# Loads in two gated bursts, w_tok's tail half first, and q of batch 1 permuted on GpSimd, in a sorted-attention and token-mixing kernel

## The chip, the cores and the metric

The kernel runs on one core of a Trainium2 chip. The metric is device microseconds of one execution. Before the change, 13 runs have a median of 261.09 us (260.26 to 266.6). The core's engines run side by side, each in its own program order, and wait for each other on semaphores: TensorE (PE) multiplies matrices into PSUM, VectorE (DVE) and ScalarE (ACT) work on SBUF and PSUM, GpSimd (POOL) works on SBUF and issues DMAs, SyncE (SP) issues DMAs.

## The reference, cut to what matters

There are 4 batches of 8 heads, 768 tokens and head dimension 64. Attention first mixes blocks of k and v with a matrix P, which five rounds of row and column normalisation of `exp(sort_net)` give, and then attends within each of 8 blocks of 96 tokens. Its output, 768 tokens by 512 channels, goes through a token-mixing step and a two-layer channel step.

```python
k_sorted = einsum('bhij,bhjcd->bhicd', P, k_b)        # and v likewise
attn = softmax(scale * q_b @ k_sb.T)                  # within a block
x = (attn @ v_sb)                                     # 768 x 512 per batch
tok = einsum('ts,bsd->btd', w_tok, alpha1 * x + beta1)
u = x + lam * tok
a2 = alpha2 * u + beta2
out = u + lam * (maximum(a2 @ w_ch1, 0) @ w_ch2)
```

## The kernel before, in words

Every engine's order of instructions is written out by hand (class `Engine`, line 56 on: what is issued through `pe`, `dve`, `act` and `pool` keeps its program order). Nearly all DMAs that load from HBM are issued by GpSimd[...]. They run as one stream, in the order in which GpSimd issues them. SP issues what is stored, the round trip of mixed v through a scratch in DRAM, and DMA transposes.

The opening works on batch 0. GpSimd issues q (two halves, `load_q0`), then k and v of the first four heads (`load_raw0`), k of the others, v of heads 4 and 5, half of w_tok (columns 0 to 383, `load_wtok(0)`), v of heads 6 and 7, the other half of w_tok, the three vectors lam, alpha1 and beta1 spread over all partitions, and then raw v of batch 1 (lines 171 to 190 and 812). Meanwhile VectorE and ScalarE make P (until 11.60 us), and TensorE turns q. Then four pairs of heads are mixed (`mix_k0`, `mix_v0`), scored (`sc0`) and applied to v (`pv0`), woven by hand.

w_tok has to be transposed. `sort_wtok(n, part)` (line 593) has GpSimd bring its columns into the order in which the blocks are cut, n being a pair of 128-wide groups: part 0 takes 96 columns of each group, from the columns 0 to 575, part 1 takes 32 of each, from the columns 576 to 767. `prep_wtok` (line 604) has TensorE turn a group, ScalarE and VectorE copying it out; `prep_rs` sums rows. Then `tok_part` multiplies the token products, six tiles of 128 tokens, `moe_scale` and `moe_rest` make u of it, `moe_turn` turns u, and `moe_h` makes the hidden layer, 16 tiles of 128 for each half of the tokens.

Batch 1 starts inside this: `mixes` mixes its v, `regroup_v` (line 378) sends it through DRAM into `Vs[1]` by two pairs of DMAs on SP, `mix_k(1)` mixes its k in three groups, and `turn_q(1, n)` (line 233) turns its q on TensorE, 12 transposes of 64 columns of weights for each pair of heads, with a copy on VectorE. These stand between tiles of `moe_h(0, 0)`. GpSimd then waits for `Vs[1]` by a small copy into the tile `gate` (line 902), and only then issues the loads of batch 2; the transposes of q of batch 2 follow on SP (`cross_q`, line 136). From there, `weave` fills the gaps between the steps of a batch's attention with channel products of the batch before (`moe_h`, `moe_ch`); `moe_a` does the next batch's token step, for which GpSimd makes u from x in `moe_rows` and `moe_start`. A tile u32 is one of 11 buffers, so a new one waits for the store of an old one.

Of the kernel before, what the change touches and what calls it, by code (L numbers as in the profile page):

```python
# [9 lines left out]
F16 = mybir.dt.float16  # L10
# [7 lines left out]
def kernel(  # L18
# [22 lines left out]
    B, H, S, D = q.shape  # L41
# [4 lines left out]
    NT = S // 128  # L46
    CT = C // 128
    HT = HID // 128
    BH = B * H
# [39 lines left out]
    def psb(shape, dtype, name):  # L89
        return psB.tile(shape, dtype, name=name, tag="psB")  # L90
# [11 lines left out]
    def load_raw(b, kv):  # L102
        src = (k, v)[kv]
        raw = att.tile([128, HB * D], F16, name=f"raw{kv}", tag=f"raw{kv}", bufs=2)
        for th in range(2):
            pool.dma_start(
                raw[th * 64:(th + 1) * 64, :],
                src[b].rearrange("h (j th t) d -> th (h j) (t d)", j=NB, th=2)[th],
            )
        raw_of[(b, kv)] = raw  # L110

    def load_raw0(kv, lo, hi):
        if lo == 0:
            raw_of[(0, kv)] = att.tile([128, H, 6, D], F16, name=f"raw{kv}", tag=f"raw{kv}", bufs=2)
        pool.dma_start(
            raw_of[(0, kv)][:, lo:hi, :, :], (k, v)[kv][0, lo:hi].rearrange("h (p x) d -> p h x d", x=6)
        )
# [25 lines left out]
    def prep_affine():  # L143
        pool.tensor_tensor(a1lB[:], a1lB[:], lamB[:], ALU.mult)
        pool.tensor_tensor(b1lB[:], b1lB[:], lamB[:], ALU.mult)
# [22 lines left out]
    def load_wtok(half):  # L168
        cols = slice(half * (S // 2), (half + 1) * (S // 2))
        pool.dma_start(wt16[:, :, cols], moe_w_tok[:, cols].rearrange("(tt p) s -> p tt s", p=128))  # L170

    load_raw0(0, 0, 4)
    load_raw0(1, 0, 4)
    load_raw0(0, 4, 8)
    load_raw0(1, 4, 6)
    load_wtok(0)
    load_raw0(1, 6, 8)
    load_wtok(1)
    ones16 = const([128, 1], F16, "ones16")
    pool.memset(ones16[:], 1.0)  # L180
    NV = 2
# [3 lines left out]
    b1lB = const([128, C], FT, "b1lB")  # L185
    lamB = const([128, C], FT, "lamB")
    gate = const([64, 2], F16, "gate")
    pool.dma_start(lamB[:], moe_lam.partition_broadcast(128))
    pool.dma_start(a1lB[:], moe_alpha1.partition_broadcast(128))
    pool.dma_start(b1lB[:], moe_beta1.partition_broadcast(128))  # L190
    W1p = const([128, CT, HID], BF, "W1p")
    W2p = const([128, HT, C], BF, "W2p")
    w1v = moe_w_ch1.rearrange("(ci p) n -> p ci n", p=128)
# [33 lines left out]
    def spin(n):  # L227
        src = ident16[:].unsqueeze(1).to_broadcast([128, 4, 128])
        for _ in range(n):
            pe.matmul(idle[:], ident16[:], src, start=True, stop=True)  # L230


    def turn_q(b, h4, copy):
        qps = psb([128, S], F16, "q_ps")
# [48 lines left out]
    def load_w1(gs):  # L283
        for g in gs:
            pool.dma_start(W1p[:, :, g * 512:(g + 1) * 512], w1v[:, :, g * 512:(g + 1) * 512])
# [302 lines left out]
    w_tokT = const([128, NT, S], F16, "w_tokT")  # L588
    rs = const([128, NT], FT, "rs")

    wtp = []

    def sort_wtok(n, part):

        if part == 0:
            wtp.append(moep.tile([128, NT, 2, 128], F16, name=f"wtp_{n}", tag="a2T", bufs=3))
        lo, hi, base = ((0, 96, 0), (96, 128, TAIL))[part]
        w = hi - lo
        pool.tensor_copy(
            wtp[n][:, :, :, lo:hi],  # L600
            wt16[:, :, base + 2 * n * w:base + (2 * n + 2) * w].rearrange("p t (k c) -> p t k c", c=w),
        )

    def prep_wtok(which):
        for ks in which:
            pst = psa([128, S], F16, "wtok_ps")
            for tt in range(NT):
                pe.transpose(pst[:, tt * 128:(tt + 1) * 128], wtp[ks // 2][:, tt, ks % 2, :], ident16[:])
            dst = w_tokT[:, ks, :].rearrange("p (kt x) -> p kt x", x=128)
            act.copy(dst[:, :, 0:96], pst[:, 0:TAIL].rearrange("p (kt x) -> p kt x", x=96))  # L610
            dve.tensor_copy(dst[:, :, 96:128], pst[:, TAIL:S].rearrange("p (kt x) -> p kt x", x=32))

    def prep_rs(rps, part):
        for ks in part:
            for kt in range(NT):
                pe.matmul(
                    rps[:, kt:kt + 1], w_tokT[:, ks, kt * 128:(kt + 1) * 128], ones16[:],
                    start=(ks + kt == 0), stop=(ks + kt == 2 * NT - 2),
                )
        if part[-1] == NT - 1:  # L620
            act.copy(rs[:], rps[:])

    u_of = {}
# [31 lines left out]
    def tok_part(b, kt):  # L655
        if b == 0 and kt == 4:
            pair = psa([128, 2, C], FT, "tok_ps")
            for n in range(2):
                tok_of[(b, kt + n)] = pair[:, n, :]
        elif (b, kt) not in tok_of:  # L660
            tok_of[(b, kt)] = psb([128, C], FT, "tok_ps")[:]
        for n, ks in enumerate((1, 4, 0, 3, 2, 5)):
            pe.matmul(
                tok_of[(b, kt)], w_tokT[:, ks, kt * 128:(kt + 1) * 128],
                x_of[b][:, ks, :], start=(n == 0), stop=(n == NT - 1),
            )
# [77 lines left out]
    def moe_h(b, hf, which=range(HT)):  # L744
        if (b, hf) not in hT_of:
            hT = moep.tile([128, HT, 384], BF, name="hT", tag=("big", "hT1")[hf], bufs=1)
            hT_of[(b, hf)] = [hT[:, m, :] for m in range(HT)]
        for m in which:
            hps = psb([128, 384], FT, "h_ps")
            for ci in range(CT):  # L750
                pe.matmul(
                    hps[:], W1p[:, ci, m * 128:(m + 1) * 128], a2T_of[b][hf][:, ci, :],
                    start=(ci == 0), stop=(ci == CT - 1),
                )
            act.activation(hT_of[(b, hf)][m], hps[:], AF.Relu)
            yield 0.65, None
# [27 lines left out]
    def run(units):  # L784
        for unit in units:
            advance(unit, 0.0)
        settle()
# [4 lines left out]
    def sc0(h4):  # L792
        pair = [psa([128, 2, 4, 128], FT, "sc_ps") for _ in range(2)]
        for g in range(2):
            score(0, h4, ((0, 1, 2, 6), (3, 4, 5, 7))[g], pair[g])
        for g in range(2):
            ets[(h4, g)] = emit_exp(pair[g])
# [11 lines left out]
    v_copy(0, dve.tensor_copy)  # L809
    v_copy(1, act.copy)  # L810
    next(big)
    load_raw(1, 1)
    sort_wtok(0, 0)
    sort_wtok(1, 0)
    load_w1((0,))
    for n, part in ((0, 1), (1, 1), (2, 0), (2, 1)):
        sort_wtok(n, part)
    load_w1((1,))
    prep_affine()
    load_w1(range(2, 4))  # L820
    load_raw(1, 0)
    sc0(0)
    for h4 in range(H4 - 1):
        turn_v0(h4, dve.tensor_copy)
        k_copy = mix_k0(h4 + 1)
        k_copy(0, act.copy)
        k_copy(1, dve.tensor_copy)
        if h4 > 0:
            pv0(h4 - 1, 0)()
        v_copy = mix_v0(h4 + 1)  # L830
        v_copy(0, dve.tensor_copy)
        v_copy(1, act.copy)
        if h4 == 0:
            next(big)
        sc0(h4 + 1)
        if h4 > 0:
            pv0(h4 - 1, 1)()
    turn_v0(3, dve.tensor_copy)
    pv0(2, 0)()
    prep_wtok(range(0, 1))  # L840
    pv0(2, 1)()
    prep_wtok(range(1, 2))
    pv0(3, 0)()
    prep_wtok(range(2, 4))
    pv0(3, 1)()
    prep_wtok(range(4, 6))
    mixing_matrices(1)
    rps = psb([128, NT], FT, "rs_ps")
    prep_rs(rps, range(4))
    moe_rows(0, (0, 1))  # L850
    moe_start(0, ())
    tok_part(0, 0)
    moe_scale(0, 0)
    prep_rs(rps, range(4, NT))
    mixes(1, 0)
    moe_rows(0, (2, 3))
    moe_start(0, range(4))
# [33 lines left out]
    mix_k(1, gs=(0,))  # L891
    run(moe_h(0, 0, range(9, 11)))
    mix_k(1, gs=(1,))
    run(moe_h(0, 0, range(11, 12)))
    turn_q(1, 0, dve.tensor_copy)
    run(moe_h(0, 0, range(12, 13)))
    mix_k(1, gs=(2,))
    for n in range(1, H4):
        run(moe_h(0, 0, range(12 + n, 13 + n)))
        turn_q(1, n, dve.tensor_copy)  # L900
    stack.close()
    pool.tensor_copy(gate[32:64, :], Vs[1][32:64, 0, 0:2])
    load_raw(2, 1)
# [10 lines left out]
    for b in range(1, B):  # L914
        if b == 1:
            fill = chain(moe_h(0, 1), moe_ch(0, 0), moe_ch(0, 1, (0,)))
            steps = [(0.2, lambda: mixing_matrices(2, psb)), (0.6, lambda: mixing_matrices(3, psb)), (0.6, lambda: None)]
            steps += attention_steps(1, 6.4, 0.3)
        else:
            fill = chain(moe_h(b - 1, 0), moe_ch(b - 1, 0), moe_h(b - 1, 1), moe_ch(b - 1, 1, (0,)))  # L920
            steps = [(g, lambda g=g, n=n: mix_k(b, gs=(n,))) for n, g in enumerate((0.6, 3.0, 3.0))]
            steps.append((3.8, lambda: None))
            steps += attention_steps(b, 5.3)
        weave(fill, steps)
        run(fill)
        moe_rows(b, range(5, NT))
        moe_a(b)
        run(moe_ch(b - 1, 1, (1, 2)))
        moe_affine(b, 1)
        if b < B - 1:  # L930
            moe_rows(b + 1, range(3))
        if b == 1:
            pool.tensor_copy(gate[32:64, :], Vs[0][32:64, 0, 0:2])
            load_raw(3, 1)
            load_raw(3, 0)
            load_q(3)
            cross_q(3, regroup[2])
        if b < B - 1:
            moe_rows(b + 1, range(3, 5))
# [33 lines left out]
```

## Time and profile before

The profiled execution took 262.57 us, of which the program's span is 260.8 us; the rest lies around it.

| engine | busy us | share of the span |
|---|---|---|
| TensorE matmul | 249.9 | 96% |
| TensorE weight load | 140.1 | 54% |
| VectorE | 147.3 | 56% |
| ScalarE | 131.6 | 50% |
| GpSimd | 94.2 | 36% |

The granted TensorE clock is 1.0 all through. The DMA moved 30.88 MB, at 118 GB/s on average over the span, and most of it in the first 66 us. Busy time of TensorE is pipelined: matmuls overlap a little, so 96% says that it seldom waits, not that it is at its peak. The chain of work that ended last gives TensorE 78% of the span, DMA 7%, VectorE 4%. In the time lines below, a DMA's row shows when it was issued and not when it landed.

### The profile page before, as it was taken

The numbers are of one execution on the slowest core, as the hardware profiler recorded it, in microseconds if no ns is written. First come the engines' busy times: TensorE is split into PE (matmuls) and PEld (weight loads), VectorE is DVE, ScalarE is ACT, GpSimd is POOL, SyncE is SP. The second block draws the span as 40 slices with busy tenths as digits, with TensorE's granted clock in tenths as the row PEclk, the third lists the DMA queues.
The fourth block names the chain that finished last, engine by engine and source line by source line (L and its number), as shares of the span: only waits on it lengthen the run. The fifth ranks groups of instructions, "written<-read, shape, count | busy, mean of one in ns | idle before, by whom it ended". The sixth has DMA issues, their size and how long they took to land.

```text
span 260.8 us, 5125 instructions
## 1 busy us (share of the span) xinstructions
PE 249.9 (96%) x2048; PEld 140.1 (54%) x2048; DVE 147.3 (56%) x324; ACT 131.6 (50%) x240; POOL 94.2 (36%) x103
## 2 busy tenths in 40 slices
PE   5988899999999989999999999999999999999993
PEld 2467745665545434654565445655665446545542
DVE  5868686592167969942626696734527963042033
ACT  3587588758623432673376542752573326505600
POOL 8525978000679098009530970222003700000000
PEclk9999999999999999999999999999999999999999
DMA  5999999999499734996995137951200341012012
GB/s 81 184 202 266 180 194 239 211 216 152 76 194 130 186 105 101 209 99 116 213 176 104 43 83 170 139 56 46 79 0 3 80 119 42 3 40 80 3 40 80
DMA packets 63127, 30.88 MB, mean 118 GB/s; under 512 B 48824, under 2 KB 58816, under 8 KB 63104
## 3 DMA queue, kind: packets, MB, share of 16 engines
q0 software_dynamic: 23712, 15.60, 41.3%
q1 hardware_dynamic: 39296, 14.90, 32.8%
q8 instruction: 16, 0.26, 0.4%
q10 hardware_dynamic: 96, 0.07, 0.1%
q14 instruction: 7, 0.06, 0.1%
HBM read 32.78 MB, written 8.65 MB: 159 GB/s over the span
## 4 chain that ended last, share of the span: by engine, by line
PE 78%; DMA 7%; DVE 4%; ACT 3%; POOL 3%; issue 2%; SPq 0%; POOLq 0%; DVEq 0%
PE h_ps L66 32%; PE ch_ps L66 30%; PE tok_ps L66 8%; DMA wt<-in_moe_w_tok_dram 7%; PE sc_ps L66 2%; PE x_ps L66 2%; DVE x L66 2%; ACT u L66 2%; PE k_ps L66 2%; POOL raw L66 1%; PE q_ps L66 1%; DMA out_dram<-u 1%; DVE u L66 1%; ACT vA L66 1%; PE v_ps L66 1%
## 5 line engine op out<-in xcount | busy, mean ns | idle before, releaser
L66 ACT ACTIVATE hT<-h_ps 128x384 bf16<-128x384 f32 x128 | 60.5, 491 | 59.5 <-PE h_ps L66 59.1
L66 PE MATMUL h_ps<-a2T,W1p 128*128 128x384 bf16 x512 | 88.9, 326 | 0.3 <-ACT a2T L66 0.2
L66 PE MATMUL ch_ps<-W2p,hT 128*128 128x512 bf16 (+2 forms) x400 | 86.9, 371 | 0.0
L66 PEld LDWEIGHTS <-W1p 128*128 128x128 bf16 x512 | 48.5, 98 | 31.9 <-issue 0.7
L66 PEld LDWEIGHTS <-hT 128*128 128x128 bf16 x400 | 37.6, 98 | 41.0
L66 DVE TENSOR_TENSOR ch_ps<-ch_ps,lamB 128x512 f32<-128x512 f32 (+2 forms) x25 | 16.9, 676 | 55.5 <-PE ch_ps L66 32.0
L66 POOL TENSOR_SCALAR u<-b1lB,rs 128x512 f32<-128x512 f32 x18 | 27.9, 1558 | 29.1 <-DMA out_dram<-u 28.9
L66 POOL TENSOR_TENSOR u<-x,u 128x512 f32<-128x512 f16 x22 | 24.9, 1162 | 31.1 <-DVE x L66 28.5
L66 PE MATMUL tok_ps<-x,w_tokT 128*128 128x512 f16 x144 | 33.2, 379 | 0.8 <-DVE u L66 0.8
L66 ACT ACTIVATE et<-sc_ps 96x768 f16<-96x768 f32 x32 | 24.0, 803 | 11.1 <-PE sc_ps L66 11.1
L66 PEld LDWEIGHTS <-w_tokT 128*128 128x128 f16 x180 | 15.0, 97 | 18.1 <-issue 1.5
L66 DVE CAST kT<-k_ps 64x512 f16<-64x512 f32 x30 | 20.6, 687 | 4.7 <-PE k_ps L66 4.3
L66 ACT CAST u<-u 128x512 f16<-128x512 f32 x24 | 14.6, 620 | 15.5 <-DVE u L66 15.5
L66 DVE RECIPROCAL recip<-x_ps 96x8 f32<-96x8 f32 (+1 forms) x32 | 6.3, 196 | 28.2 <-PE x_ps L66 28.1
L66 DVE TENSOR_TENSOR tok_ps<-tok_ps,a1lB 128x512 f32<-128x512 f32 x24 | 16.6, 696 | 4.2 <-PE tok_ps L66 4.1
L66 DVE TENSOR_TENSOR x<-x_ps,recip 96x512 f16<-96x512 f32 (+2 forms) x32 | 17.7, 555 | 1.1
L66 DVE TENSOR_TENSOR u<-tok_ps,u 128x512 f32<-128x512 f32 x24 | 15.8, 683 | 3.0 <-POOL u L66 2.7
L66 DVE TENSOR_TENSOR u<-ch_ps,u 128x512 f32<-128x512 f32 (+2 forms) x25 | 16.8, 670 | 0.9
L66 POOL DMA_DIRECT2D qn<-in_q_dram x16 | 14.0, 907 | 4.9 <-DMA raw<-in_v_dram 2.6
L66 PEld LDWEIGHTS <-et 96*128 96x128 f16 (+1 forms) x288 | 12.2, 105 | 2.7
L66 POOL COPY gate<-Vs 32x2 f16<-32x2 f16 x2 | 0.4, 176 | 35.7 <-DMA Vs<-vscr 35.7
L66 PE MATMUL x_ps<-Vs,et 96*128 96x65 f16 (+1 forms) x288 | 13.1, 197 | 0.0
(89 smaller groups left out, 183.4 us busy)
## 6 DMA issues: line engine op xcount, KB each, us to landing
out_dram<-u SPq DMA_DIRECT2D x23, 192.0 KB, 2.4
raw<-in_k_dram POOLq DMA_DIRECT2D x8, 384.0 KB, 10.9
raw<-in_v_dram POOLq DMA_DIRECT2D x7, 384.0 KB, 8.3
vscr<-vA SPq DMA_DIRECT2D x6, 384.0 KB, 5.2
Vs<-vscr SPq DMA_DIRECT2D x6, 384.0 KB, 8.4
W1p<-in_moe_w_ch_dram POOLq DMA_DIRECT2D x4, 512.0 KB, 10.5
W2p<-in_moe_w_ch_dram POOLq DMA_DIRECT2D x4, 512.0 KB, 16.0
qn<-in_q_dram POOLq DMA_DIRECT2D x4, 384.0 KB, 9.8
```

Source lines behind the costliest of these rows:

```text
L66: ins = getattr(self.eng, name)(*args, **kwargs)
```

## The change

On GpSimd's queue, only q and the first four heads of k and v are issued at once. A small copy that reads P (written by 11.60 us before) holds back the rest of k, two more heads of v, the second half of w_tok's columns and the last heads of v. A second one, which reads the exponentials of the second pair of heads, holds back the first half of w_tok's columns; the four sorts that need the second half alone come after its issue, then the three vectors, raw v of batch 1, the two other sorts, and W1. w_tok's groups are turned in the order 4, 5, 0, 1, 2, 3, and batch 0's token products and row sums follow this order. The mixing matrix of batch 1 is made in a PSUM bank of the other pool (`psb`).

q of batch 1, loaded as before, is copied by GpSimd into another order (`sort_q`, two copies, in a buffer under the tag of vA). `turn_qp` turns 128 columns of weights at a time, 6 transposes for each pair of heads. Two pairs are turned between tiles of `moe_h(0, 0)`, the two others in the first steps of the weave.

```diff
     load_raw0(0, 0, 4)
     load_raw0(1, 0, 4)
-    load_raw0(0, 4, 8)
-    load_raw0(1, 4, 6)
-    load_wtok(0)
-    load_raw0(1, 6, 8)
-    load_wtok(1)
...
-    pool.dma_start(lamB[:], moe_lam.partition_broadcast(128))
-    pool.dma_start(a1lB[:], moe_alpha1.partition_broadcast(128))
-    pool.dma_start(b1lB[:], moe_beta1.partition_broadcast(128))
+    def load_affine():
...

...
+    def sort_q(b):
+        qp_of[b] = att.tile([128, NT, H, D], F16, name="qp", tag="vA", bufs=1)
+        for hh in range(2):
+            hs = slice(4 * hh, 4 * hh + 4)
+            pool.tensor_copy(
+                qp_of[b][:, :, hs, :].rearrange("p kt h d -> p h kt d"), qn_of[b][:, hs, :, :]
+            )
+
+    def turn_qp(b, h4, copy):
+        qps = psb([128, S], F16, "q_ps")
+        for kt in range(NT):
+            pe.transpose(
+                qps[:, kt * 128:(kt + 1) * 128],
+                qp_of[b][:, kt, 2 * h4:2 * h4 + 2, :].rearrange("p h d -> p (h d)"), ident16[:],
+            )
+        copy(qT_of[b][:, h4, :, :].rearrange("p kt x -> p (kt x)"), qps[:])
...
-        for n, ks in enumerate((1, 4, 0, 3, 2, 5)):
+        for n, ks in enumerate((4, 5, 0, 1, 2, 3) if b == 0 else (1, 4, 0, 3, 2, 5)):
...
-    load_raw(1, 1)
-    sort_wtok(0, 0)
-    sort_wtok(1, 0)
-    load_w1((0,))
-    for n, part in ((0, 1), (1, 1), (2, 0), (2, 1)):
-        sort_wtok(n, part)
-    load_w1((1,))
-    prep_affine()
-    load_w1(range(2, 4))
-    load_raw(1, 0)
+    pool.tensor_copy(gate[0:BH, :], P16[:, 0, 0:2])
+    load_raw0(0, 4, 8)
+    load_raw0(1, 4, 6)
+    load_wtok(1)
+    load_raw0(1, 6, 8)
     sc0(0)
...
         sc0(h4 + 1)
+        if h4 == 0:
+            pool.tensor_copy(gate[0:64, :], ets[(1, 0)][0:64, 0, 0, 0:2])
+            load_wtok(0)
+            for n, part in ((2, 0), (2, 1), (0, 1), (1, 1)):
+                sort_wtok(n, part)
+            load_affine()
+            load_raw(1, 1)
+            sort_wtok(0, 0)
+            sort_wtok(1, 0)
+            load_w1(range(2))
+            prep_affine()
+            load_w1(range(2, 4))
+            load_raw(1, 0)
...
-    mixing_matrices(1)
+    mixing_matrices(1, psb)
...
-    run(moe_h(0, 0, range(11, 12)))
-    turn_q(1, 0, dve.tensor_copy)
-    run(moe_h(0, 0, range(12, 13)))
+    run(moe_h(0, 0, range(11, 13)))
     mix_k(1, gs=(2,))
-    for n in range(1, H4):
-        run(moe_h(0, 0, range(12 + n, 13 + n)))
-        turn_q(1, n, dve.tensor_copy)
+    sort_q(1)
+    run(moe_h(0, 0, range(13, 14)))
+    for n in range(2):
+        turn_qp(1, n, dve.tensor_copy)
+        run(moe_h(0, 0, range(14 + n, 15 + n)))
...
-            steps = [(0.2, lambda: mixing_matrices(2, psb)), (0.6, lambda: mixing_matrices(3, psb)), (0.6, lambda: None)]
+            steps = [(0.0, lambda: turn_qp(1, 2, dve.tensor_copy)), (0.6, lambda: mixing_matrices(2, psb))]
+            steps += [(0.6, lambda: turn_qp(1, 3, dve.tensor_copy)), (0.6, lambda: mixing_matrices(3, psb))]
             steps += attention_steps(1, 6.4, 0.3)
```

More of the change, by code (lines that the diff above doesn't have):

```diff
@@ L187 @@
     gate = const([64, 2], F16, "gate")
-    pool.dma_start(lamB[:], moe_lam.partition_broadcast(128))
-    pool.dma_start(a1lB[:], moe_alpha1.partition_broadcast(128))
-    pool.dma_start(b1lB[:], moe_beta1.partition_broadcast(128))
+    def load_affine():
+        pool.dma_start(lamB[:], moe_lam.partition_broadcast(128))
+        pool.dma_start(a1lB[:], moe_alpha1.partition_broadcast(128))
+        pool.dma_start(b1lB[:], moe_beta1.partition_broadcast(128))
     W1p = const([128, CT, HID], BF, "W1p")
@@ L230, in spin @@
             pe.matmul(idle[:], ident16[:], src, start=True, stop=True)
+    qp_of = {}
+    def sort_q(b):
[13 more added lines that the diff above has]
+        copy(qT_of[b][:, h4, :, :].rearrange("p kt x -> p (kt x)"), qps[:])
     def turn_q(b, h4, copy):
@@ L589 @@
     rs = const([128, NT], FT, "rs")
-    wtp = []
+    wtp = {}
     def sort_wtok(n, part):
-        if part == 0:
-            wtp.append(moep.tile([128, NT, 2, 128], F16, name=f"wtp_{n}", tag="a2T", bufs=3))
+        if n not in wtp:
+            wtp[n] = moep.tile([128, NT, 2, 128], F16, name=f"wtp_{n}", tag="a2T", bufs=3)
         lo, hi, base = ((0, 96, 0), (96, 128, TAIL))[part]
@@ L611, in prep_wtok, with prep_rs @@
             dve.tensor_copy(dst[:, :, 96:128], pst[:, TAIL:S].rearrange("p (kt x) -> p kt x", x=32))
-    def prep_rs(rps, part):
-        for ks in part:
+    def prep_rs(rps, part, first=False, last=False):
+        for n, ks in enumerate(part):
             for kt in range(NT):
@@ L617, in prep_rs @@
                     rps[:, kt:kt + 1], w_tokT[:, ks, kt * 128:(kt + 1) * 128], ones16[:],
-                    start=(ks + kt == 0), stop=(ks + kt == 2 * NT - 2),
+                    start=(first and n + kt == 0), stop=(last and n == len(part) - 1 and kt == NT - 1),
                 )
-        if part[-1] == NT - 1:
+        if last:
             act.copy(rs[:], rps[:])
@@ L839 @@
     pv0(2, 0)()
-    prep_wtok(range(0, 1))
+    prep_wtok((4,))
     pv0(2, 1)()
-    prep_wtok(range(1, 2))
+    prep_wtok((5,))
     pv0(3, 0)()
-    prep_wtok(range(2, 4))
+    prep_wtok((0, 1))
     pv0(3, 1)()
-    prep_wtok(range(4, 6))
-    mixing_matrices(1)
+    prep_wtok((2, 3))
+    mixing_matrices(1, psb)
     rps = psb([128, NT], FT, "rs_ps")
-    prep_rs(rps, range(4))
+    prep_rs(rps, (4, 5, 0, 1), first=True)
     moe_rows(0, (0, 1))
@@ L853 @@
     moe_scale(0, 0)
-    prep_rs(rps, range(4, NT))
+    prep_rs(rps, (2, 3), last=True)
     mixes(1, 0)
```

## The prediction

> **What bounds the kernel now.** I read the page's busy shares first, then the waits of TensorE after the opening, then the timeline around the one that matters, then the DMA by stretches. TensorE is busy for 96% of the span, and after 31 us it hardly waits. The list of waits (who, for whom: total us, times, longest us), TensorE only, from 30 us to the end, has four entries:
>
> ```profile
> PE tok_ps L66 <- DVE u L66: 0.8, 1, 0.8
> PE rep_ps L66 <- DVE w_tokT L66: 0.4, 1, 0.4
> PE h_ps L66 <- ACT a2T L66: 0.2, 1, 0.2
> PE wtok_ps L66 <- DVE w_tokT L66: 0.2, 1, 0.2
> ```
>
> So there are two regions: an opening of 31 us that waits for loads (the chain that ended last gives 17.54 us to the transfer of w_tok, up to 25.45), and a dense remainder with one hole of 0.77 us at 94.19. Whether a gain before 94 survives depends on that hole. The timeline (start, duration, engine, line, operation, tiles, [idle before <- releaser]) shows what ends it:
>
> ```profile
> 25.51 2.49 POOL L66 COPY wtp<-wt 128x384 f16<-128x384 f16 x4 [2.53 <-DMA wt<-in_moe_w_tok_dram]
> ...
> 48.87 0.61 PE L66 MATMUL k_ps<-bigP,raw 128*128 128x128 f16 x8
> ...
> 66.96 0.18 POOL L66 COPY gate<-Vs 32x2 f16<-32x2 f16 x1 [21.63 <-DMA Vs<-vscr]
> 67.49 1.08 POOL L66 DMA_DIRECT2D raw<-in_v_dram x2 [0.35 <-PE h_ps L66]
> ...
> 79.24 8.64 SPq L139 DMA_TRANSPOSE qT<-qn x6
> 87.98 0.52 SPq L763 DMA_DIRECT2D out_dram<-u x1
> ...
> 90.72 1.56 POOL L66 TENSOR_SCALAR u<-b1lB,rs 128x512 f32<-128x512 f32 x1 [6.45 <-DMA out_dram<-u]
> 92.25 6.78 POOL L66 TENSOR_TENSOR u<-x,u 128x512 f32<-128x512 f16 x6
> ...
> 94.19 2.75 PE L66 MATMUL tok_ps<-x,w_tokT 128*128 128x512 f16 x12 [0.77 <-DVE u L66]
> ```
>
> Read upwards. TensorE waits for VectorE's u, that for GpSimd's u at 92.25, which stands in program order behind the row at 90.72, which waits for a u buffer whose output is being stored. That store is issued at 87.98 only, because the six transposes of q of batch 2 stand before it on SP until 87.88. They began at 79.24, when that q landed, and its loads began at 67.49, after the gate on Vs of batch 1, landed at 66.82. From that landing to 94.19 it is 27.4 us of DMA, SP and GpSimd, none of which starts earlier when TensorE does. TensorE itself has 0.77 us to spare there.
>
> What sets 66.82? The DMA. By stretches (start:end, length, busy us of PE, PE's weight loads, DVE, ACT and POOL with their counts, clock, DMA share, GB/s written):
>
> ```profile
> 14.00:16.00 2.00, 1.63 (x38) 1.34 (x40) 0.85 (x3) 1.40 (x4) 0.54 (x1) 1.00 1.31 202
> 24.00:26.00 2.00, 1.23 (x28) 1.11 (x25) 1.59 (x6) 1.30 (x2) 0.49 (x2) 1.00 1.08 224
> 30.00:32.00 2.00, 1.64 (x34) 1.20 (x34) 1.50 (x7) 1.12 (x2) 2.00 (x3) 1.00 0.99 136
> 50.00:56.00 6.00, 6.00 (x72) 3.96 (x71) 5.86 (x10) 3.91 (x8) 0.00 (x0) 1.00 1.36 214
> ```
>
> The reader is to look at the last two columns: from 3 to 64 us the DMA has work without a break, and 202 GB/s, written as 16 bits from 32-bit sources, are some 404 GB/s read. The stream of loads is the second bound, running beside TensorE.
>
> **What the Trainium skill says.** *DMA: Bandwidth & Descriptors*, Specifications, puts the HBM limit of a core near 358 GB/s and the first byte of a GpSimd-issued transfer at about 1 us. The trace reads 404 GB/s, more than that; and from the issue at 67.49, with the DMA empty, its first packet starts at 68.73: 1.24 us. Its section Latency and other measured facts says that two of the sixteen DMA engines are usually slower. Agreed in kind: the trace's completion marks of v's first half come from thirteen engines at 12.1 to 12.7 and from three at 13.9 to 14.1. *GPSIMD Engine Reference*, 4.1, calls one-input operations roughly line rate; the sorts of w_tok agree (1.12 us for 1152 columns, 0.5 for 384). *TensorE: Matmul & The Clock Gate*, Part 4, gives some 275 ns for a transpose in context; here they stream at 0.67 us for 12 (uT_ps in the chain), 56 ns each, and the measurement decides.
>
> **The change part by part**, against the profiled execution (260.8 us of span, 262.57 us in all, so 1.8 us around it; the median of the runs is 261.09, 1.5 below this execution).
>
> *w_tok's order.* Now the first sort waits for w_tok's last half (25.45), and TensorE 0.84 us behind it. After, the tail half lands near 20 (its place in the stream: k's second half 1.95 us, v 0.97, w_tok 2.92, from 13.2). Sorts (2,0), (2,1), (0,1), (1,1): 1.12 + 3 x 0.5, done by 22.9. The sorts of the other half come after five DMA issues (3 x 0.55 + 2 x 0.53 = 2.7 us), 25.6 to 27.9, each before TensorE turns it, the turns taking 0.8 us apiece. So the first turn runs at 25.2 instead of 26.07: -0.87 us. ScalarE and VectorE, which copy each turn out (0.64 + 0.25), keep their pace. The bank of batch 1's mixing matrix moves from psA to psB, which ends the 0.36 us wait of rep_ps; the next token product waits for the last copy anyway: nothing.
>
> *q of batch 1.* 48 transposes of 49 ns (0.59 us for 12) become 24 of 56: 2.36 - 1.34 = -1.02 us on TensorE. VectorE's four copies stay (0.55 each), two of them moved into the weave. GpSimd gets two copies of 1536 columns, 1.4 us each by the sorts' slope, between q's landings (50.6, 52.6 now) and the first turn, about 4.8 us after the row at 48.87: 53.6. Cover is 1.6 us; without it, up to 1.4 us. They follow W2's issues and precede the gate on Vs, idle time (21.63 us) on GpSimd.
>
> So TensorE's own path gets 0.87 + 1.02 = 1.9 us shorter before 60 us, if no load is late. The product at 48.87 is the place to watch: its raw k landed at 48.73 (issued 33.21, longest landing 15.5). TensorE 0.87 earlier waits there for the same landing.
>
> *The two gates.* Each empties the stream. Gate 1 opens when P is done (11.60) and GpSimd has copied (0.2): issue at 11.9, first packet 1.24 later, 13.15. Thirteen engines ran dry near 12.0: 1.15 us x 13/16 = 0.93. Gate 2 (exp of head pair 1, about 18.5) lets the other half of w_tok out at 18.8, before the queue is empty: no gap. But behind it the affine vectors now stand after four sorts: issue 22.9, packet 24.1, while the stream ends near 22.9: 1.2 us on most engines, mean 1.0. Queued behind gate 2 on GpSimd are also raw v of batch 1, W1, the affine products and raw k. Raw v (landed 32.24, used 33.15, now wanted at 32.3) and the products (now 28.7 to 31.2, after some 29.7 to 32.2, wanted by VectorE at 32.2) just hold; W1 has 5 us in hand. k and v of gate 1's burst are wanted at 18.5 and later and land from 16. Sum +1.9 us of lost streaming. Unknown is what comes back, from 0 to all: the last engine ends Vs 1.1 us after the mean of the sixteen (65.73), and a pause lets laggards catch up, I take 0.6; the gather of Vs, issued up to 0.9 us earlier, has some 170 packets more beside W2 at 190 per us, of the 1000 per us it does alone: 0.2; the thin stretch 30 to 36 us (136 GB/s in the row above) may fill, 0 to 1.2: 0.2. I get 1.9 - 1.0 = +0.9, ends -0.7 and +1.9.
>
> *Sum.* Vs lands at 67.7, TensorE resumes near 95.1 instead of 94.19, and all after is dense: 260.8 + 0.9 = 261.7 of span, 263.5 for this execution, **262.0** on the median. The 1.9 us of TensorE become a longer wait there.
>
> **The rivals.**
> 1. *Stream on time*: laggards give everything back, Vs lands within 0.5 us of now. For: the engines that set each landing are the late ones, which the gaps don't stop. Against: 404 GB/s is a shared limit, so idle engines are lost bytes. TensorE's gain is absorbed at 94.19: 261.1.
> 2. *Faster*: evening out is worth more than the gaps cost. The mechanism is the same landing of Vs, and it decides from 66.0 down: each us earlier is a us of the end, until TensorE's own 0.77 + 1.9 is used up. For: w_tok's last engine came 1.5 us after the fifteenth (25.4, 23.9). With Vs at 65.4: 259.7.
> 3. *Slower by more*: raw k or q of batch 1 also land late (the permute then stands open, 1.4), and TensorE passes its slack: Vs +1.9 and 0.3 on top, 263.3.
> 4. *The gates do nothing*, queue never empty: as 1, for three engines it is so.
>
> **How the numbers follow.** Forecast 0.45, rival 3 0.10, rivals 1 and 4 0.25, rival 2 0.20. A difference under 0.3% (0.8 us) can't be told from none here: slower 0.55, same 0.25, faster 0.20. The forecast's own range is 261.9 to 262.9; with half of rival 2 and most of rival 3, 259.6 to 263.5.
>
> **What would show it.** Right: DMA share falling near 12 and 23 us; first wtok_ps near 25.2; q_ps of batch 1 x6; gate on Vs after 67.3; the wait of tok_ps near 95 grown to 2 us or more. Wrong: Vs by 66.0, or that wait gone; or a new TensorE wait on raw k, q or the affine vectors before 60 us that exceeds 2.7 us.

## The result and the profile after

The changed kernel takes 266.12 us (median of 11 executions, 264.63 to 267.58). Beside the kernel before, with a median of 261.81 in 48 executions, it is slower by 1.65%: ratio 1.0165, 95% interval 1.0138 to 1.0191. The prediction (262.0 us, 259.6 to 263.5) had the sign and the place of the loss, but forecast 0.9 us, where some 4.3 came. The profiled execution took 265.63 us with a span of 263.9, against 262.57 and 260.8: 3.1 us. The medians differ by more, because the profiled execution before took longer than the median of its kernel and the one after less. The two traces are therefore used for where the time goes, and the ratios for how much.

The four longest waits of TensorE from 30 us to the end (who, for whom: total us, times, longest us), changed kernel:

```profile
PE v_ps L66 <- DMA raw<-in_v_dram: 2.2, 1, 2.2
PE tok_ps L66 <- DVE u L66: 2.0, 1, 2.0
PE h_ps L66 <- DVE qT L66: 0.3, 1, 0.3
PE k_ps L66 <- DMA raw<-in_k_dram: 0.3, 1, 0.3
```

The hole before tok_ps, 0.8 before, has grown to 2.0. The prediction had named 2 us or more as a sign of being right, but by luck: it let the hole grow because TensorE comes early, and TensorE came late. Above the hole stands a wait for what the prediction said would "just hold": TensorE waits 2.2 us for raw v of batch 1. The timeline of the changed kernel (start, duration, engine, line, operation, tiles, [idle before <- releaser]), the rows that answer to those shown of before:

```profile
11.67 0.17 POOL L66 COPY gate<-P 32x2 f16<-32x2 f16 x1 [6.58 <-DVE P L66]
...
21.82 2.48 POOL L66 COPY wtp<-wt 128x1152 f16<-128x1152 f16 x4 [2.24 <-DMA wt<-in_moe_w_tok_dram]
24.25 0.57 POOL L66 DMA_DIRECT2D lamB<-in_moe_lam_dram  x1
...
70.10 0.18 POOL L66 COPY gate<-Vs 32x2 f16<-32x2 f16 x1 [13.31 <-DMA Vs<-vscr]
...
82.18 8.81 SPq L139 DMA_TRANSPOSE qT<-qn  x6
91.09 0.53 SPq L779 DMA_DIRECT2D out_dram<-u  x1
...
93.83 1.56 POOL L66 TENSOR_SCALAR u<-b1lB,rs 128x512 f32<-128x512 f32 x1 [6.66 <-DMA out_dram<-u]
```

```profile
35.49 0.59 PE L66 MATMUL v_ps<-raw,bigV 128*128 128x512 f16 x2 [2.23 <-DMA raw<-in_v_dram]
...
51.44 0.61 PE L66 MATMUL k_ps<-bigP,raw 128*128 128x128 f16 x8 [0.27 <-DMA raw<-in_k_dram]
...
97.29 2.75 PE L66 MATMUL tok_ps<-x,w_tokT 128*128 128x512 f16 x12 [1.96 <-DVE u L66]
```

The gate on Vs of batch 1 moved from 66.96 to 70.10, SP's transposes from 79.24 to 82.18, the store behind them from 87.98 to 91.09, GpSimd's sixth row from 90.72 to 93.83, and the token product behind the hole from 94.19 to 97.29: 2.9 to 3.1 us, and 3.1 is also the growth of the span. The chain that the prediction read from Vs to the hole kept its length and came 3.1 us later.

Where the loads lost it, by stretches (start:end, length, busy us of PE, PE's weight loads, DVE, ACT and POOL with counts, clock, DMA share, GB/s written). Of the kernel before, the stretch that the prediction did not show:

```profile
12.00:14.00 2.00, 1.56 (x17) 0.62 (x16) 0.97 (x3) 1.36 (x4) 0.54 (x1) 1.00 1.27 196
```

And of the changed kernel, to be set against that row and, for 14 to 16 and 24 to 26 us, against the 202 and 224 GB/s of the prediction's rows:

```profile
12.00:14.00 2.00, 1.93 (x36) 1.12 (x34) 0.74 (x3) 1.19 (x4) 2.00 (x3) 1.00 0.53 37
14.00:16.00 2.00, 1.73 (x47) 1.46 (x43) 1.34 (x4) 1.98 (x4) 0.79 (x2) 1.00 1.12 166
...
24.00:26.00 2.00, 2.00 (x54) 1.95 (x50) 1.65 (x5) 1.85 (x3) 2.00 (x5) 1.00 0.56 109
...
28.00:30.00 2.00, 1.48 (x28) 1.39 (x29) 1.18 (x4) 1.24 (x3) 2.00 (x3) 1.00 0.89 117
```

Both holes are there. Gate 1's costs (196 - 37) x 2 + (202 - 166) x 2 = 390 KB, 2.0 us at 195 GB/s; the second, before the vectors, leaves 109 of 224. A third thin stretch, 28 to 30 us, is the time in which the vectors land. The completion marks of the sixteen DMA engines give their mean: heads 6 and 7 of v at 21.6 instead of 19.7, the last half of w_tok 25.1 instead of 22.7, raw v of batch 1 34.4 instead of 28.8, Vs 69.3 instead of 65.7. For the last engine, which releases the waiting one, these are 22.8 (20.9), 27.0 (25.4), 35.4 (32.2) and 70.0 (66.8).

### The profile page after: what moved, and what is told of

The parts are those of the page before. It is cut to its first block, busy times and chain, and to the rows that moved or that the text cites. A ratio compares the mean times of both kernels' runs of the same rounds, so it can differ in the third digit from the quotient of the medians.

```text
span 263.9 us, 5084 instructions
## 1 busy us (share of the span) xinstructions
PE 249.4 (95%) x2024; PEld 140.1 (53%) x2024; DVE 147.4 (56%) x324; ACT 131.6 (50%) x240; POOL 97.6 (37%) x107
## 4 chain that ended last, share of the span: by engine, by line
PE 74%; DMA 10%; DVE 7%; POOL 4%; issue 2%; ACT 1%; POOLq 0%; SPq 0%; DVEq 0%
PE ch_ps L66 29%; PE h_ps L66 28%; PE tok_ps L66 7%; DMA raw<-in_k_dram 6%; DMA wt<-in_moe_w_tok_dram 3%; PE spin_ps L66 3%; DVE kT L66 3%; PE sc_ps L66 2%; PE x_ps L66 2%; DVE x L66 2%; PE k_ps L66 1%; POOL W1p L66 1%; ACT et L66 1%; PE q_ps L66 1%; DVE ch_ps L66 1%
## 5 line engine op out<-in xcount | busy, mean ns | idle before, releaser
L66 DVE TENSOR_TENSOR ch_ps<-ch_ps,lamB 128x512 f32<-128x512 f32 (+2 forms) x25 | 16.9, 676 | 53.9 <-PE ch_ps L66 30.4
L66 POOL TENSOR_TENSOR u<-x,u 128x512 f32<-128x512 f16 x22 | 24.9, 1162 | 31.5 <-DVE x L66 28.8
L66 PE MATMUL tok_ps<-x,w_tokT 128*128 128x512 f16 x144 | 33.2, 379 | 2.0 <-DVE u L66 2.0
L66 ACT CAST vA<-v_ps 128x1024 f16<-128x1024 f32 x9 | 9.1, 1011 | 7.3 <-PE v_ps L66 7.3
```

The lines of the kernel that those rows point to most:

```text
L66: ins = getattr(self.eng, name)(*args, **kwargs)
```

## The experiments

Two theories were to be told apart. A: holes in the stream of loads make Vs of batch 1 late, and the end follows it through stores and GpSimd's rows. B: TensorE's own waits before 62 us set the end. And within A, which of the parts makes the holes.

**Gates out, one at a time and both.**

```diff
-    pool.tensor_copy(gate[0:BH, :], P16[:, 0, 0:2])
...
-            pool.tensor_copy(gate[0:64, :], ets[(1, 0)][0:64, 0, 0, 0:2])
```

e1 leaves out the first of these lines, e2 the second, e3 both.

> The changed kernel without the copy that reads P: the second burst is issued at about 5 us, as before the change, w_tok's other half still waits for the exponentials. Theory A (the DMA stream loses what the gates and the jam of the three vectors cost, and the end follows the landing of Vs of batch 1 through the stores and GpSimd's rows): the empty stretch at 12 to 14.5 us cost 2 us of the sixteen engines' mean, so Vs lands 1.0 to 2.0 us earlier than 69.96 (68.0 to 69.0), and the ratio to the kernel before falls from 1.0165 to about 1.010. Theory B (gate 1 only evens the engines, the loss is all behind gate 2): Vs within 0.5 us of 69.96, ratio 1.015.

Measured: ratio 1.0111 (1.0052 to 1.0169). In its profile Vs landed at 69.54, only 0.4 us earlier, and TensorE waited 3.85 us for raw v of batch 1, with 0.71 left in the hole. The ratio is the one that A gave, but four executions leave an interval that overlaps the changed kernel's; that gate 1 counts is settled by e14 below. The landing forecast for Vs was missed. Of raw v the mean of the engines came 1.4 us earlier (32.97), and the last engine not (35.32 against 35.36). The profiled execution is the slowest of the four, so its waits overstate the loss.

> The changed kernel without the copy that reads the exponentials: w_tok's first half is issued behind gate 1's burst at about 15 us; the three vectors still stand behind four sorts. Theory A: the gate itself costs nothing, since the queue was not empty when it opened at 18.7; the hole at 24 to 25.5 us comes from the sorts ahead of the vectors and stays, so Vs within 0.5 us of 69.96, ratio 1.014 to 1.017. Theory B (the second gate is the loss): Vs at 68 or earlier, ratio 1.008 or less.

Measured: 1.0171 (1.0114 to 1.0227), Vs at 69.75, as A had it. Beside gate 1, gate 2 has no cost that four executions can show.

> The changed kernel without both gates, its order of loads, sorts, vectors and the permute of q kept. Theory A: without gate 1 w_tok is complete near 25, the vectors are issued after the sorts, near 24, and the hole before them shrinks; Vs at 67.5 to 68.5, ratio 1.006 to 1.010. Theory B (gates are the whole loss): Vs at 66.8 or earlier, ratio 1.000 or below, since TensorE's shorter q turns count.

Measured: 1.0102 (1.0071 to 1.0133), Vs at 68.53, the upper end of what A gave. With no gate at all a full per cent remains. The loss can't be the gates alone.

**The permute of q alone, on the kernel before.** Its edit is the permute's part of the change.

> The kernel before with the permute of q of batch 1 alone (two GpSimd copies, 24 transposes instead of 48, the new places of the turns). Theory A: TensorE gets 1.0 us shorter before 62 us, but the hole at 94 us takes it up, 0.77 growing to 1.5 to 1.8; the time stays, ratio 0.998 to 1.002. Rival (TensorE's own path sets the end): ratio 0.996, the hole unchanged. Rival (the permute is late and TensorE waits for it): a wait of q_ps on GpSimd's qp of over 0.5 us near 55.

Measured: 1.0013 (0.9985 to 1.0042): no change. In its profile, however, there is no hole at 94 at all, where one of 1.5 to 1.8 was expected; Vs landed at 65.64 there, and TensorE had lost 2.1 us between 21 and 28 us in two waits that no semaphore explains, beside 16 KB instruction fetches that began at 18.84 and 25.86. What these waits are is not shown. That the permute alone makes no difference is shown; that the hole absorbs the gain isn't shown by this trace.

**The end taken off the landing of Vs.**

```diff
     def moe_a(b):
...
-        moe_start(b)
+        if b == 1:
+            moe_start(b, range(5))
+            moe_rows(b, (5,))
+            moe_start(b, (5,))
+        else:
+            moe_start(b)
...
-        moe_rows(b, range(5, NT))
+        if b > 1:
+            moe_rows(b, range(5, NT))
         moe_a(b)
```

> The changed kernel with one edit far from the change: in batch 1's token step GpSimd adds x to five rows of u before it makes the sixth row, which waits for a store, so that the hole near 97 us no longer hangs on the landing of Vs. Theory A (the end follows Vs through stores and rows): the hole of 1.96 goes, and the end comes 1.5 to 2.0 us earlier, ratio about 1.009; what is left is TensorE's own lateness from raw v of batch 1. Rival (TensorE's own waits before 62 us set the end): no change, 1.0165, the hole only moves or stays.

Measured: 1.0092 (1.0067 to 1.0117), span 261.1. The waits of TensorE from 30 us on in this run are all but one small (the three longest):

```profile
PE v_ps L66 <- DMA raw<-in_v_dram: 1.6, 1, 1.6
PE h_ps L66 <- DVE qT L66: 0.3, 1, 0.3
PE h_ps L66 <- ACT hT L66: 0.2, 1, 0.2
```

The tok_ps row is gone, although Vs landed as late as before (69.67). So 0.7%, some 1.9 us, was what the chain from Vs cost beyond TensorE's own path, as A had it. The 0.9% that this edit doesn't touch agrees with lateness of TensorE's own: in this trace, the shortest of 20 executions, its first scores of batch 1 come at 61.42, 1.3 us later than before. A holds, and B stands right behind it; the prediction had B at nil.

> The kernel before with the one edit in batch 1's token step alone (five rows of u get x before the sixth row is made). If the hole at 94 us hangs on the landing of Vs through stores and rows, it goes and with it 0 to 0.8 us, according to how large it is in the run: ratio 0.997 to 1.000. If the hole has another cause it stays and the ratio is 1.000.

Measured: 1.0006 (0.9982 to 1.0030); no hole, with Vs at 65.16. On the kernel before the edit makes no difference that can be measured, so what e9 gained is not a gain of the edit by itself. That Vs is mostly early enough there for the hole to cost little would explain it; the other executions have no trace that shows it.

**The vectors and raw v of batch 1.** In e5 and e6 the vectors are issued right behind w_tok's first half; e6 leaves out both gates as well.

```diff
             load_wtok(0)
+            load_affine()
             for n, part in ((2, 0), (2, 1), (0, 1), (1, 1)):
                 sort_wtok(n, part)
-            load_affine()
```

> The changed kernel with the three vectors issued straight behind w_tok's first half, ahead of the four sorts (at 19.6 us instead of 24.25); raw v of batch 1 still behind the sorts. Theory A (hole and jam of the vectors behind the sorts are the larger part of the loss): no hole at 24 to 25.5, b1lB lands near 28.5 instead of 31.36, raw v of batch 1 near 33 instead of 35.36, TensorE's wait for it falls from 2.23 to under 0.7, Vs at 68 to 68.7, ratio 1.008 to 1.011. Rival (gate 1 is all that matters): raw v and Vs within 0.5 us of the changed kernel's, ratio 1.015 or more.

Measured: 1.0117 (1.0022 to 1.0212). The interval holds both answers, and the profiled execution (269.30 us) is the slowest of the four and is not read. Inconclusive by itself.

> The changed kernel with both gates out and the vectors ahead of the sorts: what is left of the change is the order of w_tok's halves, raw v of batch 1 behind four sorts, and the permute. Theory A: the stream has no hole any more, Vs at 66.8 to 67.5, TensorE waits for raw v under 0.5 us, ratio 1.000 to 1.004. Rival (the order of w_tok's halves or the permute costs something itself): ratio over 1.006.

Measured: 1.0000 (0.9970 to 1.0030), Vs at 66.12, even earlier than expected, no wait for raw v, which landed at 30.00. This is the decisive run: the order of w_tok's halves and the permute of q, which it keeps, together cost nothing, and the whole loss lies in when the loads are issued. Against e3 only the place of the vectors differs: without gates, vectors behind the sorts cost 1.0%. Its waits show what the prediction had expected of the changed kernel:

```profile
PE tok_ps L66 <- DVE u L66: 1.6, 1, 1.6
PE k_ps L66 <- DMA raw<-in_k_dram: 1.2, 1, 1.2
```

TensorE waits for raw k of batch 1 near 48, still comes to batch 1's first scores 1.3 us earlier than before (58.91), and the hole takes the gain.

> The changed kernel with the three vectors' tiles filled from 128 different rows of the second channel matrix each, instead of one row read 128 times: the same bytes, the same issues, another result (the affine part is left out and replaced by these numbers). If all engines reading one row at once is what makes the third vector take 2.5 us, it lands within 1.3 us of the second, raw v of batch 1 near 33.8, TensorE's wait for it under 1.0, ratio about 1.011. If it is the refilling of an empty queue, or anything else, the vectors land as before (27.8, 28.8, 31.4) and the ratio stays at 1.0165.

Measured: 1.0160 (1.0094 to 1.0226). The third vector landed 1.46 us after the second instead of 2.54, at 29.3 instead of 31.4: most of what the theory of one row had (under 1.3). But the last engine of raw v landed at 34.78, TensorE waited 1.88 us, and the time did not move by anything that four executions can show. So reading one row from everywhere does slow the third vector, and is not the main part of what makes raw v late.

> The changed kernel with raw v of batch 1 issued ahead of the three vectors, both still behind gate 2 and the four sorts. The theory that raw v, queued behind the vectors, makes TensorE's own lateness: raw v lands near 31.5 instead of 35.36, TensorE does not wait for it (under 0.4 instead of 2.23), mixed v is stored about 2 us earlier; but the vectors come 3 us later, near 33.5, their products on GpSimd near 36, and VectorE's first scaling of a token product waits for them, so that TensorE stands still for PSUM instead: ratio 1.014 to 1.020. Rival (raw v's place does not matter, only the bytes lost): Vs and the ratio unchanged within 0.2%, with no new wait.

Measured: 1.0188 (1.0135 to 1.0241). Raw v landed at 32.23 and TensorE didn't wait for it. The wait moved to VectorE, which stood still for the products of the vectors (timeline of this run, VectorE):

```profile
34.76 0.70 DVE L66 TENSOR_TENSOR tok_ps<-tok_ps,a1lB 128x512 f32<-128x512 f32 x1 [2.04 <-POOL a1lB L66]
36.38 1.42 DVE L66 SCALAR_TENSOR_TENSOR u<-b1lB,rs,x 128x512 f32<-128x512 f32 x2 [0.92 <-POOL b1lB L66]
```

and Vs landed at 70.58; mixed v was stored at 40.58, as late as in the changed kernel (40.72). Which of the two comes first makes little difference: behind the sorts, both are too late.

**Gates back, with the vectors ahead of the sorts.** Each is e6 with one gate's line put back.

> The kernel without gates and with the vectors ahead of the sorts (ratio 1.000), with gate 1 put back. Theory: gate 1's price is its own, the empty stretch at 12 to 14.5 us, whatever the vectors do: Vs 1 to 2 us later than 66.12, ratio 1.004 to 1.007, as it was between the changed kernel and the one without gate 1. Rival (with the vectors ahead, the evened engines make up for the stretch): ratio within 0.003 of 1.000.

Measured: 1.0104 (1.0070 to 1.0137), median 263.64. Gate 1 has a price of its own, more than the 0.4 to 0.7% of the theory. Vs landed at 67.77; raw k of batch 1 at 49.73, for which TensorE waited 1.61 us. The stretch is the same as in the changed kernel:

```profile
12.00:14.00 2.00, 1.87 (x28) 0.94 (x28) 0.99 (x4) 1.36 (x4) 2.00 (x3) 1.00 0.50 36
```

> The kernel without gates and with the vectors ahead of the sorts, with gate 2 put back: w_tok's first half and the vectors are issued at 18.2 us instead of 8 to 14. Theory: the queue still holds some data then, so gate 2 alone costs nothing: ratio 0.998 to 1.003. Rival (it lets the stream run short as gate 1 does): ratio over 1.004, with a thin stretch near 20 us.

Measured: 1.0070 (1.0048 to 1.0092), median 263.35. The rival holds here. Without gate 1 the queue runs dry while gate 2 is shut:

```profile
18.00:20.00 2.00, 2.00 (x51) 1.61 (x50) 1.79 (x5) 1.50 (x4) 1.74 (x4) 1.00 0.66 96
```

96 GB/s, where the kernel before moved 202. Its profiled execution, 261.99 us against a median of 263.35, is the shortest of 22, so the trace shows the thin stretch and not the loss that follows.

In one table, ratio to the kernel before:

| | no gate | gate 1 | gate 2 | both |
|---|---|---|---|---|
| vectors ahead of the sorts | 1.0000 | 1.0104 | 1.0070 | 1.0117 (wide) |
| vectors behind the sorts | 1.0102 | 1.0171 | 1.0111 | 1.0165 |

The causes don't add up. Each alone costs 0.7 to 1.0%, and gate 2 adds nothing clear of the noise where gate 1 or the sorts have already made the same loads late.

**A version that beats both.** e12 is e6 with the edit in the token step; e13 also issues raw k of batch 1 ahead of W1's last quarter; e16 is e13 with the old turns of q.

```diff
-            load_w1(range(2, 4))
-            load_raw(1, 0)
+            load_w1((2,))
+            load_raw(1, 0)
+            load_w1((3,))
```

> Both gates out, the vectors ahead of the sorts, and the edit in batch 1's token step; w_tok's order and the permute of q stay. If the hole at 94 us (1.64 in that kernel without the edit) swallows TensorE's gain, it now comes through: 1.2 to 1.8 us, ratio 0.993 to 0.996; TensorE still waits about 1 us for raw k of batch 1 near 48. Rival (another wait takes its place at once): ratio 0.998 or more.

Measured: 260.37 us, 0.9944 (0.9926 to 0.9963). The hole is gone; TensorE waits 0.64 for raw k.

> As the run before, with raw k of batch 1 issued ahead of the last quarter of W1. If raw k's landing is what TensorE waits for near 48, it lands near 45 and the wait of 1.0 to 1.3 goes, ratio 0.989 to 0.993; the last quarter of W1 lands near 48, needed near 49. Rival (W1's last quarter is late in its place, or q's permute, or Vs itself for the first product with v near 69): ratio 0.994 or more, with a wait of that name.

Measured: 259.27 us, 0.9923 (0.9900 to 0.9946). Raw k landed at 44.39 instead of 48.03, W1's last quarter at 47.74, and nothing over 0.3 us is left from 30 us on:

```profile
PE h_ps L66 <- DVE qT L66: 0.3, 1, 0.3
PE h_ps L66 <- ACT hT L66: 0.2, 1, 0.2
PE h_ps L66 <- ACT a2T L66: 0.2, 1, 0.2
```

> The fastest kernel so far (0.9923: no gates, vectors ahead of the sorts, raw k ahead of W1's last quarter, five rows of u before the sixth), with the old turns of q of batch 1 in place of the permute. If TensorE's path sets the end there, the permute is worth what TensorE saves, 1.0 us less the 0.6 us of new small waits near 55: ratio 0.994 to 0.997. Rival (another stream sets the end and hides it): ratio 0.9915 to 0.9935.

Measured: 260.03 us, 0.9949 (0.9925 to 0.9972). The ratio lies in the first of the two ranges expected. The medians differ by 0.76 us, more than the 0.4 that TensorE's 1.0 less 0.6 gave, but they were not measured side by side and the two intervals overlap, so that the permute helps is likely and not shown.

## Why the prediction was right and wrong, step by step

**The chain from Vs to the hole at 94: right.** Its marks moved by 2.9 to 3.1 us, and cutting it (e9) brought back 0.7%. The eleven traces that have this hole show how it works with TensorE's own path. TensorE comes to the product 33.2 to 33.3 us after batch 1's first scores, and the product starts 27.0 to 28.0 us after the gate on Vs, whatever TensorE did; the later of the two decides. Before, TensorE was there at 93.4 and the chain let it go on at 94.2; in the changed kernel it was 95.3 and 97.3. So the 3.1 us by which the span grew are the lateness of Vs, and TensorE's own 1.9 us lie hidden behind them until the chain is cut.

**"1.9 - 1.0 = +0.9": the step that failed for the time.** Vs landed 3.1 us later. The place of both holes was right and their sizes were not. Gate 1 was put at 0.93 us of mean stream and took 2.0. The gap itself was as forecast: on the mean the first burst ended at 12.33, and the refilled queue's first packet came at 13.25. But the prediction let the stream resume at full rate from there, and by stretches of one us it did not (changed kernel):

```profile
13.00:14.00 1.00, 0.93 (x26) 0.70 (x24) 0.29 (x2) 0.41 (x2) 1.00 (x2) 1.00 0.74 26
14.00:15.00 1.00, 0.73 (x24) 0.54 (x20) 0.99 (x3) 0.97 (x3) 0.79 (x2) 1.00 0.93 127
15.00:16.00 1.00, 1.00 (x25) 0.92 (x25) 0.36 (x1) 1.00 (x2) 0.00 (x0) 1.00 1.31 204
```

The first packets took up to 1.02 us each, against 79 ns in steady flow, as had those at the very start of the kernel before (0.93; 33 GB/s from 2 to 4 us), where it could have been seen. The second hole was put at 1.0. The last half of w_tok fell to 25.1 on the mean, 2.4 late, and the vectors added 2.9 more (30.4 against 25.1 for the third). Of these 2.9 the prediction had only the pause: it let the vectors' own transfer take no longer than before. Behind the sorts, with the sixteen engines on the same row together, the third vector landed 2.5 us after the second, and e11 shows that a part of this, 1.1, comes from the row. So raw v, behind all of this, is 5.6 us late on the mean (34.4 against 28.8), where the sum said 1.9.

The Trainium skill's *DMA: Bandwidth & Descriptors*, Specifications, gives the first byte of a GpSimd-issued transfer as about 1 us, and the prediction reckoned with the trace's 1.24 us. Both tell when data begins, and neither tells how long a queue takes to come up to its rate; of gate 1's 2.0 us that was about half.

What comes back was put at 1.0 of 1.9. The laggards did catch up: on raw v the mean is 5.6 us later and the last engine 3.1. The thin stretch from 30 to 36 us did fill, with (198 + 197 + 207 - 136 - 175 - 188) x 2 = 206 KB more than before, about 1 us. At Vs the mean is 3.5 later and the last engine 3.1. The laggards' part was only 0.4 there, instead of 0.6, and an earlier gather gave nothing, since mixed v was stored 2.3 us later and not 0.9 earlier. More came back than forecast, but of a loss three times as large.

**"TensorE's own path gets 1.9 us shorter": the other step that failed, with the sentence that raw v "just holds".** The first token product began at 31.53, the same as before (31.55): the first turn of w_tok came at 25.65 instead of the forecast 25.2, after a wait of 0.75 us at 20.8 that no semaphore explains, and a later one waited 0.43 us for a sort. Then TensorE waited 2.23 us for raw v of batch 1. The prediction held raw v to its old landing of 32.24, while adding 1.9 us of holes to the stream in which raw v stands behind both. It landed at 35.36. The same 1.9 us were charged to Vs and not to what comes 30 us before it; the list of signs of being wrong had raw k, q and the vectors, but not raw v. At batch 1's first scores TensorE was 1.9 us late (62.08 against 60.16) where it had been forecast to be early.

**q of batch 1: right in its size, hidden.** Six transposes take 0.34 us, where twelve took 0.59. New waits of 0.24, 0.09 and 0.28 us near 59 to 60 stand against it, the first put down to ScalarE's hT and the last to VectorE's qT; VectorE now copies q behind ten copies of mixed k, and the prediction had these copies at nothing. (The 275 ns that the prediction cites is the time of one transpose, for which the trace of before has 219 ns; its 56 ns are the time from one transpose to the next.) The permute took 1.46 us for each half on GpSimd, as estimated, and TensorE didn't wait for it.

**Rivals.** The faster case needed Vs by 66.0; no run with a gate had it. Raw k of batch 1 as a new wait, named for the case of "slower by more", is real in e6 and e14 (1.2, 1.6 us), but in the changed kernel it was small (0.27), with TensorE itself late. That the gates do nothing is refuted by the stretch from 12 to 14 us. Against the first rival stood that 404 GB/s is a shared limit: that idle engines are lost bytes came true (v of heads 6 and 7 1.9 us late on the mean), but no run here shows where a limit lies.

## What to carry to other kernels

A gate that emptied a busy DMA queue cost its gap and the time to refill; and every load behind it was late, not just the last one of a chain. So, when a stream of loads is charged with a delay, go down its order and set each landing against the time at which its user wants it, nearest slack first. When one late stream feeds two paths to the end, the later one sets it, and cutting that one gives back only its lead over the other: here 1.9 us of 4.3.

## What the runs showed that was not expected

- A refilled DMA queue began with packets of up to 1.02 us, where 79 ns is usual, and from its first packet at 13.25 moved 26 GB/s to 14, 127 to 15 and 204 to 16 us. Gate 1 alone was worth 1.0% (e14), for a gap of 0.9 us on the mean.
- Three vectors, each one row spread over 128 partitions, took 31.4 - 24.25 = 7.1 us from the first issue to the last landing when all engines reached them together. With 128 different rows (e11) it was 29.3 - 24.15 = 5.1 us, and the time of the kernel stayed.
- Delays of one stream did not add. Two gates and the vectors' place cost 1.0, 0.7 and 1.0% each alone, and 1.65% together.

A wait of TensorE can cost more than its length. In the traces of e1, e2, e3 and e11 the granted clock falls to a half for 3.4 us, each time 1.2 to 1.4 us after TensorE went on from a wait of 2.06 to 3.85 us. In e2 that is after the hole at 97:

```profile
97.17 4.01 PE L66 MATMUL tok_ps<-x,w_tokT 128*128 128x512 f16 x12 [2.06 <-DVE u L66]
```

```profile
98.50:102.00 3.50, 3.28 (x9) 1.23 (x9) 3.27 (x6) 1.70 (x3) 3.50 (x5) 0.51 0.44 100
```

The twelve products take 4.01 us there and 2.75 in the changed kernel's trace, and from their start to the end it is 168.2 to 168.3 us in e2 and e11, against 166.6 in the traces of before and of the changed kernel. No trace in which all of TensorE's waits after 18 us were under 2 us shows such a stretch before TensorE's last product; the changed kernel's trace, with 2.23 and 1.96, has none either, so the wait alone doesn't decide it, and what does is not shown. The mean clock of the changed kernel was 0.994 or less in 8 of 12 executions, that of the kernel before in 5 of the 43 that stood beside e15, that of e12, e13 and e16 in none of 47. So a part of what the waiting kernels lose may be this; how much is not separated here.
